# Retention and two dense layers on one core: a list scheduler with measured occupancies, a delay per engine, and VectorE that waits for GpSimd in its model

## The chip, the cores and the metric

The kernel runs on one core of one Trainium2 chip. The time is device microseconds of an execution of the program. Engines are TensorE (PE in the profile, its weight loads PEld), VectorE (DVE), ScalarE (ACT), GpSimd (POOL) and SyncE (SP), which issues every DMA.

## The reference

```python
# q, k, v: 4 batches x 8 heads x 576 positions x 64, float32
scores = (q @ k.T) / sqrt(64)
ret    = scores * gamma[h] ** (i - j)   (for i >= j, else 0)
x      = (ret @ v), heads side by side          # 2304 x 512
h = x @ w_in                                    # 512 x 2048
x = (h * tanh(log1p(exp(min(h, 20))))) @ w_out  # first layer
h = maximum(x @ w_in2, 0)
out = (h * h) @ w_out2                          # second layer
```

## The kernel before

**Stages.** Attention first: 20 steps (4 batches, each of 4 chunks of 128 positions and a tail of 64). A step has products `sc` (scores, line 394), `st` (state, 415) and `o` (438 and 446); VectorE multiplies the scores by a mask (402) and the output by a decay into `part` (464), ScalarE copies the state into `sbd`. Then the two layers. Each runs 4 passes over its hidden columns and in each pass 3 visits, one for 768 tokens. A visit has two rounds; a round makes the hidden block of 256 columns by seven products P1 to P7 (line 589, banks `h`) of 6 matmuls each, in the manner of Strassen, and `y_group` (639, banks `py`) multiplies activated blocks by the output weights.

**Numbers are split.** A float32 operand is kept as two tiles, a rounded part and the rest, and a product takes three matmuls. ScalarE writes the rounded part and another engine subtracts it to get the rest; that is a *split*. The splits of activations (`g`, line 237, always on VectorE) stand between `h` and `py`. The splits of weights (`win`, `wout`) and of the layer's input (`ring`) go through `either` (lines 229 to 231).

**Weights.** They arrive as 64-bit words in `raw`, two tiles in turn. `convert` (249) makes 32-bit floats of a block of 128 x 512: ScalarE forms `y` from the low words, VectorE masks, clamps and shifts the high words into `z` (261, 262, 263), puts the sign into `y` (264), and an integer add of `z` and `y` (265) ends it. Two `z` tiles are used in turn.

**After a product.** ScalarE copies a bank to `cp`, VectorE adds it to another bank (line 572) into a bank or, for P7, into the SBUF tile `e`. In the first layer ScalarE applies mish; in the second ScalarE takes a relu and VectorE multiplies (548). Then the split into `g`. When all columns of a pass are done, VectorE adds `py` to `part` (662). Between layers `sums_x` (317 to 319) and 324 form differences of blocks of `part`, and `split_x` fills the seven `ring` tiles, which `keep` writes to DRAM and `fetch` brings back for later passes.

**The planner.** No order is written out by hand. Every operation is first recorded in `Plan` with an engine, a cost and the names that it reads and writes. `due` gives each a latest time, counted back from TensorE's order; `order` then runs a list schedule over five queues, and the kernel is issued in the order of the planned starts. Each engine works its own queue strictly in that order. Some operations are shared (`ANY`): VectorE or GpSimd may take them (the integer add, the splits of weights and input), or ScalarE too (the scaling of v, line 380). Before the change VectorE takes a shared operation only when it is due within `SOON` of its start:

```python
                if e == "DVE":
                    c = [i for i in c if len(ops[i][0]) == 1 or due[i] + lag < max(free[e], ready[i]) + SOON]
```

One delay `LAT` stands between any two engines, and an engine's own results are free.

Of the kernel before, what the change touches and what calls it, by code (L numbers as in the profile page):

```python
# [19 lines left out]
DM = H * D  # L20
# [30 lines left out]
LAT = 0.2  # L51
AHEAD = 14
BACKLOG = 4.0
SOON = 2.0
# [3 lines left out]
class Plan:  # L58

# [12 lines left out]
    def add(self, eng, cost, fn, reads=(), writes=(), moved=0.0):  # L72
        i = len(self.ops)
        deps = set()
        for k in reads:
            deps.update(self.wrote.get(k, ()))
        for k in writes:
            deps.update(self.wrote.get(k, ()))
            deps.update(self.read.get(k, ()))
        deps.discard(i)  # L80
        for k in writes:
            self.wrote[k], self.read[k] = [i], []
        for k in reads:
            if k not in writes:
                self.read.setdefault(k, []).append(i)
        costs = cost if eng == "ANY" else {eng: cost}
        self.ops.append((costs, fn, sorted(deps), moved))
        return i

    def due(self):  # L90
        due = [1e9] * len(self.ops)
        t = 0.0
        for i, (costs, _, _, _) in enumerate(self.ops):
            if "PE" in costs:
                due[i] = t
                t += costs["PE"]
        for i in range(len(self.ops) - 1, -1, -1):
            for d in self.ops[i][2]:
                costs, _, _, moved = self.ops[d]
                c = min(costs.values()) + (moved + 2.0 if "SP" in costs else 0.0)  # L100
                due[d] = min(due[d], due[i] - c - LAT)
        return due

    def order(self):
# [21 lines left out]
        queue = lag = 0.0  # L126
        for _ in range(n):
            best = None
            while first < len(pe) and done_pe[first]:
                first += 1  # L130
            for e in self.ENGINES:
                c = waiting[e]
                if e == "PE":
                    c = [i for i in c if at[i] < first + AHEAD]
                if not c:
                    continue
                if e == "DVE":
                    c = [i for i in c if len(ops[i][0]) == 1 or due[i] + lag < max(free[e], ready[i]) + SOON]
# [10 lines left out]
            costs, fn, deps, moved = ops[i]  # L149
            for e in costs:  # L150
                waiting[e].remove(i)
            if eng == "PE":
                done_pe[at[i]] = True
                lag = now - due[i]
            start[i], on[i] = now, eng
            end = free[eng] = now + costs[eng]
            if eng == "SP":
# [11 lines left out]
    def issue(self, engines):  # L169
        for i in self.order():  # L170
            costs, fn, _, _ = self.ops[i]
            fn(engines[self.on[i]]) if len(costs) > 1 else fn()
# [3 lines left out]
def kernel(  # L176
# [45 lines left out]
    def act(out, in_, func=AF.Copy, n=512, reads=(), writes=(), **kw):  # L222
        fn = lambda: nc.scalar.activation(out() if callable(out) else out, in_() if callable(in_) else in_, func, **kw)  # L223
        plan.add("ACT", 0.2 + n * 0.00084, fn, reads, writes)
# [24 lines left out]
    def convert(i, after=()):  # L249
# [11 lines left out]
        dve(lambda: ts(z, hi, 0x7FFFFFFF, None, op0=band), 600, [kr + (1,)], [kz])  # L261
        dve(lambda: ts(zf, zf, HI_MIN, HI_MAX, op0=ALU.max, op1=ALU.min), 400, [kz], [kz])  # L262
        dve(lambda: ts(z, z, 3, None, op0=shl), 400, [kz], [kz])  # L263
        dve(lambda: stt(yu, hi, 0x80000000, yu, op0=band, op1=bor), 450, [kr + (1,), ky], [ky], True)  # L264
        add = lambda eng: eng.tensor_tensor(yu, z, yu, op=ALU.add)  # L265
        plan.add("ANY", dict(DVE=0.15 + DM * 0.0017, POOL=0.2 + DM * 0.0024), add, [kz, ky], [ky])
# [100 lines left out]
    def scale_v(s):  # L367
# [15 lines left out]
        plan.add("ANY", dict(DVE=1.2, POOL=1.25, ACT=2.1), fn, ["vdec", kl], [kl])  # L383
# [153 lines left out]
    def activate(m, key, ph, kp):  # L537
# [5 lines left out]
        else:  # L543
# [5 lines left out]
                TH, [kp, ("e", l)], [kp],  # L549
# [4 lines left out]
            TH, [kp, ("g", j, 0)], [("g", j, 1)],  # L554
        )

    def chain(u, fp):
# [18 lines left out]
        def product(name):  # L576
# [19 lines left out]
            plan.add("PE", 1.045, mm, [kw + (0,), kw + (1,), ("x", i, 0), ("x", i, 1), kb], [kb])  # L596
# [23 lines left out]
    def y_group(u, th, f):  # L620
# [7 lines left out]
        for i in range(na):  # L628
# [16 lines left out]
            plan.add("PE", 0.52 if m == 0 else 0.68, mm, [kw + (0,), kw + (1,), ("g", j, 0), ("g", j, 1), ky], [ky])  # L645
# [139 lines left out]
```

## Time and profile before

| | us |
|---|---|
| median of 3 runs | 867.67 (863.89 to 868.24) |
| the profiled execution | 865.53 |
| its span, first to last instruction | 863.8 |
| TensorE busy | 834.6 (97%) |
| VectorE, ScalarE, GpSimd busy | 594.7, 429.4, 296.8 |
| attention, to the first `h` product | 91.6 |

Busy time is what the records of an engine cover; matmul records overlap a little, and their ends are modelled. A record of VectorE is longer than its share of the engine's time by the overlap with the next one, some 0.1 us. The chain of waits names for each moment the work that the end hung on.

### The profile page before, as it was taken

How to read it: one execution, taken by the hardware profiler on the slowest of the kernel's cores; microseconds unless marked ns; L12 is line 12 of the kernel's file. 1: busy time of each engine (PE TensorE's matmuls, PEld its weight loads, DVE VectorE, ACT ScalarE, POOL GpSimd, SP SyncE). 2: the span in 40 equal slices, each digit the busy share in tenths (PEclk: the TensorE clock that was granted, in tenths of full speed). 3: DMA queues.
4: the chain of work that ended last, by engine and by line, in shares of the span. 5: the costliest groups of instructions: out<-in, count | busy, mean ns of one | idle time of the engine just before them, and what ended most of it. 6: DMA issues, size and time to landing. Idle time of an engine off the chain costs nothing.

```text
span 863.8 us, 13279 instructions
## 1 busy us (share of the span) xinstructions
PE 834.6 (97%) x5067; PEld 781.8 (91%) x5067; DVE 594.7 (69%) x969; ACT 429.4 (50%) x901; POOL 296.8 (34%) x194
## 2 busy tenths in 40 slices
PE   8789999999999999999999979999999999999998
PEld 6677898999999999999999868989889899889986
DVE  4999978557447853687469988678568874664553
ACT  4766675665345533553355646565344533443331
POOL 0655766444014401351039837442023411320000
PEclk9998999999999999999999989999999999999999
DMA  9999556377357547467528455468348546426621
GB/s 317 356 317 362 182 234 232 137 291 296 127 208 287 199 197 263 165 235 300 203 79 304 129 225 225 166 267 320 126 164 309 202 172 254 178 108 263 262 104 74
DMA packets 48079, 190.87 MB, mean 221 GB/s; under 512 B 9488, under 2 KB 11664, under 8 KB 48016
## 3 DMA queue, kind: packets, MB, share of 16 engines
q1 hardware_dynamic: 48016, 190.03, 59.2%
q8 instruction: 40, 0.66, 0.3%
q14 instruction: 23, 0.19, 0.1%
HBM read 152.26 MB, written 37.75 MB: 220 GB/s over the span
## 4 chain that ended last, share of the span: by engine, by line
PE 82%; DVE 12%; DMA 3%; issue 2%; ACT 1%; POOL 0%; SPq 0%; DVEq 0%; ACTq 0%; POOLq 0%
PE py L639 42%; PE h L589 36%; DMA qk<-in_qk_dram 2%; DVE z L261 2%; DVE z L262 1%; DVE y L264 1%; DVE g L237 1%; DVE z L263 1%; DMA qk<-in_qk_t_dram 1%; PE sc L394 1%; PE o L446 1%; PE o L438 1%; DVE a L402 1%; DVE part L662 1%; DVE part L324 1%
## 5 line engine op out<-in xcount | busy, mean ns | idle before, releaser
L589 PE MATMUL h<-ring,win 128*128 128x384 f32 x2016 | 385.7, 337 | 5.6 <-DVE e L572 2.1
L589 PEld LDWEIGHTS h<-ring,win 128*128 128x128 f32 x2016 | 356.4, 188 | 16.8 <-ACT cp L223 2.6
L639 PE MATMUL py<-wout,g 128*128 128x512 f32 x864 | 217.2, 396 | 5.7 <-DVE g L237 5.7
L639 PE MATMUL py<-g,wout 128*128 128x384 f32 x1152 | 215.1, 334 | 0.0
L639 PEld LDWEIGHTS py<-g,wout 128*128 128x128 f32 x1152 | 201.2, 188 | 0.2 <-DVE g L237 0.2
L639 PEld LDWEIGHTS py<-wout,g 128*128 128x128 f32 x864 | 162.2, 189 | 35.8 <-DVE g L237 6.1
L223 ACT ACTIVATE cp<-h 128x384 f32<-128x384 f32 x144 | 70.8, 492 | 135.9 <-PE h L589 134.9
L265 POOL TENSOR_TENSOR y<-z,y 128x512 uint32<-128x512 uint32 x64 | 87.3, 1365 | 145.7 <-DVE z L263 109.5
L230 POOL TENSOR_TENSOR win<-y,win 128x512 fp32r<-128x512 f32 x32 | 43.1, 1347 | 242.3 <-ACT win L223 242.3
L237 DVE TENSOR_TENSOR g<-h,g 128x384 fp32r<-128x384 f32 x144 | 78.9, 551 | 40.9 <-ACT g L223 40.8
L572 DVE TENSOR_TENSOR h<-h,cp 128x384 f32<-128x384 f32 x96 | 54.0, 562 | 55.7 <-PE h L589 52.2
L223 ACT ACTIVATE g<-h 128x384 fp32r<-128x384 f32 x144 | 70.6, 491 | 37.1 <-DVE h L548 35.0
L572 DVE TENSOR_TENSOR e<-h,cp 128x384 f32<-128x384 f32 x48 | 26.7, 556 | 82.8 <-ACT cp L223 82.8
L662 DVE TENSOR_TENSOR part<-py,part 128x384 f32<-128x384 f32 (+1 forms) x126 | 74.4, 611 | 9.2 <-PE py L639 7.8
L230 POOL TENSOR_TENSOR ring<-part,ring 128x768 fp32r<-128x768 f32 x30 | 61.5, 2061 | 10.2 <-ACT ring L223 10.1
L264 DVE SCALAR_TENSOR_TENSOR y<-raw,y 128x512 uint32<-128x512 uint32 x64 | 61.3, 961 | 2.8 <-ACT y L223 2.6
L223 ACT ACTIVATE h<-h 128x384 f32<-128x384 f32 x72 | 34.4, 478 | 53.4 <-DVE h L572 37.4
L223 ACT ACTIVATE e<-h 128x384 f32<-128x384 f32 x72 | 35.3, 490 | 51.4 <-DVE h L572 35.7
L237 DVE TENSOR_TENSOR g<-e,g 128x384 fp32r<-128x384 f32 x48 | 44.1, 919 | 21.0 <-ACT g L223 20.8
L230 POOL TENSOR_TENSOR wout<-y,wout 128x512 fp32r<-128x512 f32 x32 | 45.8, 1435 | 36.4 <-ACT wout L223 35.3
L548 DVE SCALAR_TENSOR_TENSOR h<-h,e 128x384 f32<-128x384 f32 x72 | 40.4, 561 | 20.0 <-ACT e L223 19.6
L223 ACT ACTIVATE y<-raw 128x512 f32<-128x512 uint32 x64 | 42.9, 672 | 18.2 <-POOL wout L230 6.1
(45 smaller groups left out, 668.9 us busy)
## 6 DMA issues: line engine op xcount, KB each, us to landing
ring<-d SPq DMA_DIRECT2D x126, 768.0 KB, 6.7
raw<-in_wp_dram SPq DMA_DIRECT2D x64, 512.0 KB, 5.7
d<-ring SPq DMA_DIRECT2D x42, 768.0 KB, 5.0
kv<-in_kv_dram SPq DMA_DIRECT2D x16, 512.0 KB, 7.1
qk<-in_qk_dram SPq DMA_DIRECT2D x16, 512.0 KB, 6.7
out_dram<-part SPq DMA_DIRECT2D x18, 256.0 KB, 2.0
qdec_sb<-in_qdec_dram SPq DMA_DIRECT2D x4, 256.0 KB, 7.9
qk<-in_qk_t_dram SPq DMA_DIRECT2D x4, 256.0 KB, 8.3
```

The lines of the kernel that those rows point to most:

```text
L223: fn = lambda: nc.scalar.activation(out() if callable(out) else out, in_() if callable(in_) else in_, func, **kw)
L230: fn = lambda eng: eng.tensor_tensor(out, a, b.bitcast(F32), op=op)
L237: return lambda: eng.tensor_tensor(out, a, b.bitcast(F32), op=ALU.subtract)
L261: dve(lambda: ts(z, hi, 0x7FFFFFFF, None, op0=band), 600, [kr + (1,)], [kz])
L262: dve(lambda: ts(zf, zf, HI_MIN, HI_MAX, op0=ALU.max, op1=ALU.min), 400, [kz], [kz])
L264: dve(lambda: stt(yu, hi, 0x80000000, yu, op0=band, op1=bor), 450, [kr + (1,), ky], [ky], True)
L265: add = lambda eng: eng.tensor_tensor(yu, z, yu, op=ALU.add)
L548: lambda: nc.vector.scalar_tensor_tensor(ph(), ph(), 0.0, e(), op0=ALU.max, op1=ALU.mult),
L572: lambda: nc.vector.tensor_tensor(dst(), bank(b)(), late["cp"][j], op=ALU.add),
L589: nc.tensor.matmul(dst(), w[:, hw, wi, s], ring[i][:, hx, k], start=(new and k == 0 and n == 0), stop=(k == 1 and n == 2), skip_group_chec ...
L639: nc.tensor.matmul(y, st[:, a], mv[:, b], start=(f == 0 and k == 0), stop=(f == FPP - 1 and k == 2), skip_group_check=True,)
L662: lambda dst=dst, y=y: nc.vector.tensor_tensor(dst, y(), dst, op=ALU.add),
```

## The change

The costs that the planner works with become occupancies (`0.07 + n * 0.00104` for any VectorE operation, `0.09 + n * 0.00084` for ScalarE). The one delay becomes one for each producing engine, `SEEN`, and only TensorE's own results are free. An operation may carry a mark `port`: it reads SBUF alone on VectorE. In the model such an operation starts on VectorE no earlier than 0.1 us ahead of the end of GpSimd's current one, and when VectorE chooses, a marked operation's due time is raised by that wait. The test with `SOON` and `lag` goes: VectorE may take a shared operation at any time, with its due time raised by `SPARE`.

```diff
-LAT = 0.2
+SEEN = dict(PE=0.2, ACT=0.15, DVE=0.13, POOL=0.1, SP=0.1)
-SOON = 2.0
+SPARE = 1.5
...
-                c = min(costs.values()) + (moved + 2.0 if "SP" in costs else 0.0)
-                due[d] = min(due[d], due[i] - c - LAT)
+                e = min(costs, key=costs.get)
+                c = costs[e] + SEEN[e] + (moved + 2.0 if e == "SP" else 0.0)
+                due[d] = min(due[d], due[i] - c)
...
-                if e == "DVE":
-                    c = [i for i in c if len(ops[i][0]) == 1 or due[i] + lag < max(free[e], ready[i]) + SOON]
-                    if not c:
-                        continue
...
-                i = min(can) if e == "PE" else min(can, key=lambda i: (due[i], i))
+                if e == "PE":
+                    i = min(can)
+                elif e == "DVE":
+                    held = max(0.0, free["POOL"] - now)
+                    i = min(can, key=lambda i: (due[i] + held * ops[i][4] + SPARE * (len(ops[i][0]) > 1), i))
+                else:
+                    i = min(can, key=lambda i: (due[i], i))
...
+            if eng == "DVE" and port:
+                now = max(now, free["POOL"] - 0.1)
             end = free[eng] = now + costs[eng]
...
-                ready[u] = max(ready[u], end + (0.0 if eng in ops[u][0] else LAT))
+                ready[u] = max(ready[u], end + (0.0 if eng == "PE" and "PE" in ops[u][0] else seen))
...
-        plan.add("DVE", 0.15 + n * (0.0017 if sbuf else 0.00105), fn, reads, writes)
+        plan.add("DVE", 0.07 + n * 0.00104, fn, reads, writes, port=sbuf)
...
-        plan.add("ANY", dict(DVE=0.15 + n * 0.0017, POOL=0.2 + n * 0.0024), fn, reads, writes)
+        plan.add("ANY", dict(DVE=0.07 + n * 0.00104, POOL=0.15 + n * 0.0024), fn, reads, writes, port=True)
...
-        plan.add("ANY", dict(DVE=0.15 + DM * 0.0017, POOL=0.2 + DM * 0.0024), add, [kz, ky], [ky])
+        plan.add("ANY", dict(DVE=0.6, POOL=1.4), add, [kz, ky], [ky], port=True)
...
-        plan.add("ANY", dict(DVE=1.2, POOL=1.25, ACT=2.1), fn, ["vdec", kl], [kl])
+        plan.add("ANY", dict(DVE=0.6, POOL=1.4, ACT=2.0), fn, ["vdec", kl], [kl], port=True)
```

The costs of the conversion's passes and of two TensorE operations change by small amounts too. The order of the instructions changes throughout. Lines of the changed kernel are one higher than those of the one before.

**VectorE in the first layer.** From an `h` add to the next `e` add, in the second visit; `z` are passes for later weight blocks, `ring` and L324 belong to the next input. Before:

```order
L572 TENSOR_TENSOR h<-h,cp 128x384
L261 TENSOR_SCALAR z<-raw 128x512
L262 TENSOR_SCALAR z<-z 128x512
L263 TENSOR_SCALAR z<-z 128x512
L237 TENSOR_TENSOR g<-h,g 128x384 x2
L261 TENSOR_SCALAR z<-raw 128x512
L262 TENSOR_SCALAR z<-z 128x512
L263 TENSOR_SCALAR z<-z 128x512
L324 TENSOR_TENSOR part<-part,t_96 128x2x384
L572 TENSOR_TENSOR e<-h,cp 128x384
```

after the change:

```order
L573 TENSOR_TENSOR h<-h,cp 128x384
L231 TENSOR_TENSOR ring<-part,ring 128x768
L238 TENSOR_TENSOR g<-h,g 128x384
L325 TENSOR_TENSOR part<-part,t_96 128x2x384
L231 TENSOR_TENSOR ring<-t_96,ring 128x768
L573 TENSOR_TENSOR e<-h,cp 128x384
```

The six passes on `z` have moved ahead of the `h` add, and two ring splits, which were GpSimd's, stand in their place.

**VectorE where the first layer goes over into the second.** From the last difference for the input (L324, now L325) to the second of two `h` adds. Before:

```order
L324 TENSOR_TENSOR part<-part,t_96 128x2x384
L572 TENSOR_TENSOR e<-h,cp 128x384
L264 SCALAR_TENSOR_TENSOR y<-raw,y 128x512
L263 TENSOR_SCALAR z<-z 128x512
L548 SCALAR_TENSOR_TENSOR e<-e 128x384
L548 SCALAR_TENSOR_TENSOR h<-h,e 128x384
L261 TENSOR_SCALAR z<-raw 128x512
L237 TENSOR_TENSOR g<-e,g 128x384
L237 TENSOR_TENSOR g<-h,g 128x384
L572 TENSOR_TENSOR h<-h,cp 128x384
```

after the change:

```order
L325 TENSOR_TENSOR part<-part,t_96 128x2x384
L573 TENSOR_TENSOR e<-h,cp 128x384
L231 TENSOR_TENSOR ring<-t_97,ring 128x768
L549 SCALAR_TENSOR_TENSOR h<-h,e 128x384
L549 SCALAR_TENSOR_TENSOR e<-e 128x384
L238 TENSOR_TENSOR g<-h,g 128x384
L573 TENSOR_TENSOR h<-h,cp 128x384
L318 TENSOR_TENSOR t_97<-part 128x768
L238 TENSOR_TENSOR g<-e,g 128x384
```

The passes on `y` and `z` between the `e` add and the `g` split from `e` have gone further down; a ring split has come in, and the wide difference `t_97` now stands ahead of the `g` split from `e`.

**GpSimd at the same place**, with the numbers of the tiles. Before:

```order
L230 TENSOR_TENSOR ring_75<-part_69,ring_75 128x768
L230 TENSOR_TENSOR ring_77<-t3_97,ring_77 128x768
L230 TENSOR_TENSOR ring_78<-part_69,ring_78 128x768
L230 TENSOR_TENSOR ring_74<-part_69,ring_74 128x768
L230 TENSOR_TENSOR win_80<-sums_95,win_80 128x768
L230 TENSOR_TENSOR win_80<-y_92,win_80 128x512
L265 TENSOR_TENSOR y_94<-z_90,y_94 128x512
L230 TENSOR_TENSOR wout_81<-y_93,wout_81 128x512
L265 TENSOR_TENSOR y_91<-z_89,y_91 128x512
L265 TENSOR_TENSOR y_92<-z_90,y_92 128x512
L230 TENSOR_TENSOR wout_82<-y_94,wout_82 128x512
L230 TENSOR_TENSOR wout_83<-y_91,wout_83 128x512
```

after the change:

```order
L231 TENSOR_TENSOR ring_76<-t2_96,ring_76 128x768
L231 TENSOR_TENSOR ring_75<-part_69,ring_75 128x768
L231 TENSOR_TENSOR ring_78<-part_69,ring_78 128x768
L231 TENSOR_TENSOR win_80<-y_92,win_80 128x512
L231 TENSOR_TENSOR ring_74<-part_69,ring_74 128x768
L231 TENSOR_TENSOR wout_81<-y_93,wout_81 128x512
L266 TENSOR_TENSOR y_91<-z_89,y_91 128x512
L231 TENSOR_TENSOR wout_82<-y_94,wout_82 128x512
L231 TENSOR_TENSOR wout_83<-y_91,wout_83 128x512
```

Between the same tiles `ring_75` and `wout_83` one ring split, a split of `sums` and two integer adds are no longer GpSimd's at this place.

## Rows read from the trace of the kernel before

**Rows 1.** Table by stage; columns: stretch, length, then busy time (instructions) by engine.
```profile
50.00:75.00 25.00, 20.52 (x289) 17.57 (x289) 24.29 (x35) 13.03 (x36) 13.36 (x10) 0.90 0.99 365
91.00:106.00 15.00, 12.99 (x71) 11.90 (x70) 14.87 (x21) 9.60 (x19) 12.40 (x8) 1.00 0.40 127
130.00:148.00 18.00, 15.95 (x92) 15.63 (x91) 15.43 (x16) 9.53 (x18) 12.31 (x7) 1.00 0.73 277
148.00:450.00 302.00, 302.00 (x1735) 302.00 (x1734) 184.07 (x329) 146.73 (x292) 85.10 (x60) 0.99 0.57 214
450.00:503.00 53.00, 46.72 (x255) 43.79 (x253) 52.21 (x59) 31.48 (x58) 48.96 (x26) 0.97 0.62 226
530.00:859.00 329.00, 329.00 (x1630) 295.26 (x1629) 209.42 (x368) 143.13 (x289) 75.13 (x51) 1.00 0.53 201
```

**Rows 2.** Chain of waits in order of time: start, length, what.
```profile
91.62 2.37 PE h L589 x12
...
154.31 2.08 PE h L589 x12
...
582.74 2.08 PE py L639 x9
...
849.76 8.90 PE py L639 x39
```

**Rows 3.** Groups by line and shape, TensorE: busy, mean | idle before.
```profile
L589 PE MATMUL h<-ring,win 128*128 128x384 f32 x2016 | 385.7, 337 | 5.6 <-DVE e L572 2.1 <-DVE g L237 1.5 <-ACT cp L223 1.3
...
L639 PE MATMUL py<-wout,g 128*128 128x512 f32 x864 | 217.2, 396 | 5.7 <-DVE g L237 5.7
L639 PE MATMUL py<-g,wout 128*128 128x384 f32 x1152 | 215.1, 334 | 0.0
```

**Rows 4.** TensorE in order of time: start, length, group [idle before].
```profile
147.25 4.98 PE L589 MATMUL h<-ring,win 128*128 128x384 f32 x18 [2.05 <-DVE e L572]
...
502.92 4.21 PE L639 MATMUL py<-wout,g 128*128 128x512 f32 x9 [5.74 <-DVE g L237]
```

**Rows 5.** Groups by line and shape, VectorE and GpSimd.
```profile
L237 DVE TENSOR_TENSOR g<-h,g 128x384 fp32r<-128x384 f32 x144 | 78.9, 551 | 40.9 <-ACT g L223 40.8
...
L230 POOL TENSOR_TENSOR ring<-part,ring 128x768 fp32r<-128x768 f32 x30 | 61.5, 2061 | 10.2 <-ACT ring L223 10.1
...
L264 DVE SCALAR_TENSOR_TENSOR y<-raw,y 128x512 uint32<-128x512 uint32 x64 | 61.3, 961 | 2.8 <-ACT y L223 2.6
...
L263 DVE TENSOR_SCALAR z<-z 128x512 uint32<-128x512 uint32 x64 | 44.1, 689 | 0.9
L237 DVE TENSOR_TENSOR g<-e,g 128x384 fp32r<-128x384 f32 x48 | 44.1, 919 | 21.0 <-ACT g L223 20.8
```

**Rows 6.** VectorE in order of time, between the layers.
```profile
451.64 1.49 DVE L290 TENSOR_TENSOR sums<-y,sums 128x256 f32<-128x256 f32 x1
...
494.21 2.06 DVE L263 TENSOR_SCALAR z<-z 128x512 uint32<-128x512 uint32 x1
...
500.24 2.15 DVE L237 TENSOR_TENSOR g<-e,g 128x384 fp32r<-128x384 f32 x1
...
503.73 0.94 DVE L317 TENSOR_TENSOR t<-part 128x768 f32<-128x768 f32 x1
```

**Rows 7.** VectorE in order of time, first layer.
```profile
128.96 0.69 DVE L264 SCALAR_TENSOR_TENSOR y<-raw,y 128x512 uint32<-128x512 uint32 x1
...
134.90 0.57 DVE L572 TENSOR_TENSOR h<-h,cp 128x384 f32<-128x384 f32 x1 [0.96 <-PE h L589]
...
145.44 0.43 DVE L263 TENSOR_SCALAR z<-z 128x512 uint32<-128x512 uint32 x1
...
146.65 0.55 DVE L572 TENSOR_TENSOR e<-h,cp 128x384 f32<-128x384 f32 x1
```

**Rows 8.** VectorE and TensorE in order of time, attention.
```profile
66.67 3.96 DVE L261 TENSOR_SCALAR z<-raw 128x512 uint32<-128x512 uint32 x1
...
72.91 2.08 PE L394 MATMUL sc<-qk 64*128 64x128 f32 x16 [0.50 <-DMA qk<-in_qk_dram]
```

More of the change, by code (lines that the diff above doesn't have):

```diff
@@ L70, in __init__, with add @@
         self.ops, self.wrote, self.read = [], {}, {}
-    def add(self, eng, cost, fn, reads=(), writes=(), moved=0.0):
+    def add(self, eng, cost, fn, reads=(), writes=(), moved=0.0, port=False):
         i = len(self.ops)
@@ L86, in add @@
         costs = cost if eng == "ANY" else {eng: cost}
-        self.ops.append((costs, fn, sorted(deps), moved))
+        self.ops.append((costs, fn, sorted(deps), moved, port))
         return i
@@ L92, in due @@
         t = 0.0
-        for i, (costs, _, _, _) in enumerate(self.ops):
+        for i, (costs, *_) in enumerate(self.ops):
             if "PE" in costs:
@@ L98, in due @@
             for d in self.ops[i][2]:
-                costs, _, _, moved = self.ops[d]
-                c = min(costs.values()) + (moved + 2.0 if "SP" in costs else 0.0)
-                due[d] = min(due[d], due[i] - c - LAT)
+                costs, _, _, moved, _ = self.ops[d]
+                e = min(costs, key=costs.get)
+                c = costs[e] + SEEN[e] + (moved + 2.0 if e == "SP" else 0.0)
+                due[d] = min(due[d], due[i] - c)
         return due
@@ L125, in order @@
                 release(i)
-        queue = lag = 0.0
+        queue = 0.0
         for _ in range(n):
@@ L148, in order @@
             now, i, eng = best
-            costs, fn, deps, moved = ops[i]
+            costs, fn, deps, moved, port = ops[i]
             for e in costs:
@@ L153, in order @@
                 done_pe[at[i]] = True
-                lag = now - due[i]
             start[i], on[i] = now, eng
+            if eng == "DVE" and port:
+                now = max(now, free["POOL"] - 0.1)
             end = free[eng] = now + costs[eng]
+            seen = SEEN[eng]
             if eng == "SP":
@@ L170, in issue @@
         for i in self.order():
-            costs, fn, _, _ = self.ops[i]
+            costs, fn, *_ = self.ops[i]
             fn(engines[self.on[i]]) if len(costs) > 1 else fn()
@@ L223, in act @@
         fn = lambda: nc.scalar.activation(out() if callable(out) else out, in_() if callable(in_) else in_, func, **kw)
-        plan.add("ACT", 0.2 + n * 0.00084, fn, reads, writes)
+        plan.add("ACT", 0.09 + n * 0.00084, fn, reads, writes)
     def dve(fn, n, reads, writes, sbuf=False):
-        plan.add("DVE", 0.15 + n * (0.0017 if sbuf else 0.00105), fn, reads, writes)
+        plan.add("DVE", 0.07 + n * 0.00104, fn, reads, writes, port=sbuf)
     def either(op, out, a, b, n, reads, writes):
         fn = lambda eng: eng.tensor_tensor(out, a, b.bitcast(F32), op=op)
-        plan.add("ANY", dict(DVE=0.15 + n * 0.0017, POOL=0.2 + n * 0.0024), fn, reads, writes)
+        plan.add("ANY", dict(DVE=0.07 + n * 0.00104, POOL=0.15 + n * 0.0024), fn, reads, writes, port=True)
     def dma(out, in_, reads, writes, size):
@@ L595, in product @@
             kb = ("h", banks[b])
-            plan.add("PE", 1.045, mm, [kw + (0,), kw + (1,), ("x", i, 0), ("x", i, 1), kb], [kb])
+            plan.add("PE", 1.041, mm, [kw + (0,), kw + (1,), ("x", i, 0), ("x", i, 1), kb], [kb])
             if name == "P1":
@@ L643, in mm @@
                     )
-            plan.add("PE", 0.52 if m == 0 else 0.68, mm, [kw + (0,), kw + (1,), ("g", j, 0), ("g", j, 1), ky], [ky])
+            plan.add("PE", 0.52 if m == 0 else 0.69, mm, [kw + (0,), kw + (1,), ("g", j, 0), ("g", j, 1), ky], [ky])
         if f < FPP - 1:
```

12 lines of the change are left out of this document (6 added, 6 removed).

## Prediction

> **What bounds the kernel now.** I read the table by stage first, then the chain of waits, then the rows of the engines where those two point. From 148 to 450 us and from 530 to 859 us TensorE is busy without a gap and VectorE only six tenths of the time [rows 1]: nothing that VectorE or GpSimd do there moves the end. Three other stretches of the two layers lose time, and each has VectorE busy nearly throughout: 91 to 106 (14.87 of 15 us), 130 to 148 (15.43 of 18) and 450 to 503 (52.21 of 53) [rows 1].
>
> How much is lost follows from rates. In the chain an undisturbed group of 12 h products takes 2.08 us, 0.1733 each, and 9 of the wide py products take 2.08, 0.2311 each [rows 2]. With the counts of [rows 3], (2016 + 1152) x 0.1733 + 864 x 0.2311 = 748.7 us. The two layers run from 91.62 to 858.66, the end of the last py group [rows 2], so 767.0 us: 18.3 are lost. At 147.25 TensorE had waited 2.05 us and then ran 18 products in 4.98 instead of 3.12 us [rows 4]: 3.9. Idle time from 450 to 503 is 6.3 us [rows 1], of it 5.74 in one wait that ends at 502.92, with a group of 9 at 4.21 instead of 2.08 behind it [rows 4]: 8.4, and about 3.5 more in small pieces up to 530. Some 2.5 us are left for 91 to 106.
>
> Why VectorE is late there is in the length of its rows. A shift of a weight block takes 0.43 us at 145.44 [rows 7] and 2.06 at 494.21; the g split that reads e takes 2.15 at 500.24 [rows 6]. Long rows read SBUF alone; the g split averages 0.92 us from e and 0.55 from h, which lies in PSUM [rows 5]. The long ones end where a GpSimd instruction ends, and GpSimd was busy 48.96 of these 53 us [rows 1]. So VectorE is **held** while GpSimd works. Between 451.64 and 500.24 I count 22 held instructions (first and last in [rows 6]) that take 24 us beyond their shortest rows, of the 52 us that VectorE was busy. A held instruction is no loss by itself; the loss is that adds and splits that TensorE needs stand behind it in VectorE's order.
>
> **The change part by part.** *Moved work.* Counted in the program's order, 59 of 190 instructions leave GpSimd and 58 reach VectorE (9 ring, 24 win and 8 wout splits, 17 integer adds; one v scaling goes to ScalarE). Priced by their groups, 2.06 us for a ring split [rows 5] and 1.35 to 1.9 for the others, GpSimd loses about 93 us, near a third of its time.
>
> What an integer add costs on VectorE no row shows: it is a custom instruction over 1024 two-byte elements. The bounds are 0.69 us, a two-input pass of 512 four-byte elements that is not held [rows 7], and 1.25, the 0.94 of a 768-wide pass [rows 6] scaled to 1024. I take 0.7, since the bytes are those of 512 words, and keep 1.25 for the range. Splits go by the same rows: 0.95 for 768 elements, 0.69 for 512.
>
> *450 to 530* carries most of the sum. From the first ring split of this visit to the last of the next, GpSimd's order has 24 instructions before and 16 after. If held time goes with their number, 24 x 16 / 24 = 16 us are left: 8 saved. VectorE's own work for the same stretch of TensorE's order hardly changes, 27.4 before and 27.0 us after by unheld prices: four splits come in, and passes for later weight blocks go out behind the g splits. Between the e add and the g split from e stood three weight passes; after, a ring split and one wide difference stand there, and no weight pass. VectorE's 52 us become about 43.5, and TensorE needs 43 for these products: the 5.74 us wait shrinks to about 1, and the slow group behind it goes (2.1). What is deferred comes back: behind 503 VectorE's own work rises by 1 to 4 us with as much on GpSimd as before, so those small pieces stay and may grow by 1. Gain 7, from 3 (half the held time stays) to 10.
>
> *130 to 148.* Between the h add at 134.9 and the e add that starts at 146.65 [rows 7] stood six weight passes, with five ring splits on GpSimd beside them; after the change no weight pass stands there but two ring splits on VectorE, with two on GpSimd. Own work 3.8 us and at most two holds of 2: under 8 against 11.7. Wait and slow clock should go: 3.5 of 3.9, at worst 1.
>
> *91 to 106.* Own work goes from 9.7 to 8.9 us, GpSimd's from 13.5 to 12.9 by shortest prices. Gain 1, from 0 to 2.
>
> *0 to 91, attention.* VectorE is busy 24.29 of 25 us [rows 1], so every moved instruction shows. Four more shared ones run on it, 3.0 us (4.2 at the upper price); GpSimd goes from 28 instructions to 24, the fewer ones mostly between 60 and 78, where one pass was held 3.96 us and TensorE ran a 16-product group at 2.08 [rows 8], at about half speed. Held time saved is 3 to 4 us, and 4 more if the slow clock goes. Against that, the DMA share is 0.99 from 50 to 75 [rows 1], and SP's order has eight weight blocks and six ring copies ahead of the last attention loads both before and after; the swap of the first two loads hides behind the mask's landing. I take 2 us gained, from 3 lost to 5 gained.
>
> *Delays and occupancies* add no instruction; they act through these orders. Small new waits somewhere: 1.5 us lost.
>
> Sum: 2 + 1 + 3.5 + 7 - 1.5 = 12 us off the profiled execution's 865.5: 853.5. That execution lies 2 us below the median of the three runs, which spread over 4.4; for the median after I say **854.5**.
>
> The Trainium skill speaks against such a move: "Perfetto Trace Analysis", section "Optimizing Scalar/DVE Operations", says that GpSimd and VectorE share a port under an exclusive lock, so that offloading between the two might not help. By that rule nothing is gained and the time stays near 865.
>
> Sums over the program look like that too. The three SBUF groups of [rows 5] alone are held 54 us beyond their shortest rows, all such groups about 107, that is 0.36 per us of GpSimd; 93 us less there frees some 34, and the moved work costs 45 to 54 on VectorE. I go by the stretches, where 16 replace 24 at equal own work, and not by the average; the trade is the first rival.
>
> **Rivals.** *VectorE trades held time for own work and stays late.* For it: the sums just given, and more than half of GpSimd's loss lies where TensorE is saturated anyway. Against it: VectorE's own work from 450 to 503 does not rise. Then the place at 130 to 148 improves and the one behind 503 worsens by about as much, and the median's own offset of 2 stays: 862 to 867, say 864.5.
>
> *Moved instructions are held themselves.* 17 of them stand in the stretches from 91 to 160 and 450 to 560. If each takes what held rows take, 2.1 us [rows 6], that is 36 us of VectorE in front of adds for TensorE, against a third of some 38 held, 12.6. VectorE has perhaps 14 us to spare in them, so the end moves out by 9: 875, **slower**. It decides from about 1.6 us per moved instruction, where 27 equals 12.6 and the spare time. For it: rows of 2 us are common. Against it: the planner now adds the rest of GpSimd's instruction to the due time of work that would be held, so other work goes ahead.
>
> *All of it.* The three stretches lose nothing and attention gains 4: 18.3 + 4 less 1 off, 844 to 848.
>
> **How the numbers follow.** The forecast, 848 to 861 by its bounds, has 0.56; all of it 0.12; the trade 0.23; slower 0.09. About 0.5% (4.3 us) is what a measurement can tell from no change, so faster means below 863.3. The forecast, the full case and a quarter of the trade are that: 0.74. The rest of the trade is within: 0.17. The range, 846 to 867, leaves out the slow case and most of the full one.
>
> **What would show it.** Right: the wait before the py group near 500 falls below 2 us; held instructions on VectorE from 450 to 500 fall from 22 to about 15; the wait before 18 h products near 145 is gone; GpSimd's busy time is near 205 us; the first h product starts between 87 and 92. An integer add at 0.7 confirms the price, 1.25 the upper one. Wrong: splits on VectorE that average over 1.6 us; the same wait, only later, at 510 to 560; a first h product after 95; gaps between 148 and 450, where I expect none.

## The result and the profile after

The change takes 857.12 us (median of 4 runs, 856.17 to 858.28) against 867.13 (863.89 to 868.24): a ratio of 0.9891 [0.9861, 0.9922], faster by 1.1%. (The numbers in brackets are a 95% interval.) The profiled execution took 856.53, 9.0 less than that of before. Its table by stage, with the columns of [rows 1]:

```profile
25.00:50.00 25.00, 21.55 (x273) 18.76 (x274) 22.80 (x34) 23.16 (x71) 18.93 (x11) 0.86 1.01 370
91.00:106.00 15.00, 13.05 (x75) 12.85 (x76) 12.63 (x20) 8.67 (x18) 10.75 (x8) 0.77 0.27 78
130.00:148.00 18.00, 18.00 (x105) 18.00 (x105) 14.34 (x24) 11.25 (x22) 3.73 (x2) 1.00 0.58 222
148.00:450.00 302.00, 302.00 (x1745) 302.00 (x1744) 193.99 (x357) 145.99 (x289) 44.72 (x32) 1.00 0.59 219
450.00:503.00 53.00, 52.57 (x285) 49.80 (x284) 52.93 (x66) 33.83 (x64) 33.68 (x18) 1.00 0.62 238
503.00:530.00 27.00, 25.90 (x129) 22.96 (x128) 25.16 (x35) 16.63 (x31) 20.87 (x12) 1.00 0.54 212
```

TensorE's idle time from 130 to 148 is gone, and from 450 to 503 it is 0.43 us (before 6.28, [rows 1]). Over the program GpSimd is busy 212.3 us instead of 296.8. But VectorE is as busy from 450 to 503 as it was: 52.93 for 52.21. TensorE's waits in the layers (start, length, group, idle before it and what ended that) are short now, where [rows 4] had 5.74:

```profile
94.67 13.14 PE L590 MATMUL h<-ring,win 128*128 128x384 f32 x60 [1.35 <-DVE part L465]
...
495.66 2.31 PE L640 MATMUL py<-wout,g 128*128 128x512 f32 x9 [0.30 <-DVE g L238]
...
528.40 2.34 PE L640 MATMUL py<-wout,g 128*128 128x512 f32 x9 [1.10 <-DVE g L238]
```

The first row is the other side of the account: the first `h` product starts at 94.67, not at 91.62 [rows 2], and its 60 matmuls take 13.14 us where 60 x 0.1733 = 10.4 would do; the granted clock from 91 to 106 averages 0.77 of full speed, so that TensorE ran part of this stretch at the lower of its two levels (1.2 GHz instead of 2.4). The chain's last row gives the end of the layers:

```profile
840.75 8.90 PE py L640 x39
```

So the layers run from 94.67 to 849.65, 755.0 us: 6.3 above the 748.7 that the counts need, where 18.3 were lost before. Gained in the layers 12.0, lost in attention 3.05: the 9.0. Each of these figures comes from one execution of each kernel; how far executions differ in attention is told in the last section. The groups that answer to [rows 5], and that of the moved integer adds (busy, mean ns):

```profile
L265 DVE SCALAR_TENSOR_TENSOR y<-raw,y 128x512 uint32<-128x512 uint32 x64 | 54.5, 852 | 3.0 <-ACT y L224 3.0
L264 DVE TENSOR_SCALAR z<-z 128x512 uint32<-128x512 uint32 x64 | 37.4, 587 | 1.1
L238 DVE TENSOR_TENSOR g<-e,g 128x384 fp32r<-128x384 f32 x48 | 34.2, 712 | 21.2 <-ACT g L224 21.2
L266 DVE CUSTOM_DVE_ANT_0 y<-z,y 128x1024 uint16<-128x1024 uint16 x17 | 14.2, 834 | 0.5
```

Rows are held less, but not much less: from 450 to 503 I count 18 held ones with 19.8 us beyond their shortest rows, where it was 22 with 24. From 450 to 530 it is 28 us, and 27 before: there nothing was saved. That the layers became 12 us shorter all the same is what the experiments had to explain.

### The profile page after: what moved, and what is told of

The parts are those of the page before. It is cut to its first block, busy times and chain, and to the rows that moved or that the text cites. A ratio compares the mean times of both kernels' runs of the same rounds, so it can differ in the third digit from the quotient of the medians.

```text
span 854.7 us, 13229 instructions
## 1 busy us (share of the span) xinstructions
PE 835.0 (98%) x5067; PEld 784.9 (92%) x5067; DVE 608.4 (71%) x1027; ACT 431.6 (50%) x909; POOL 212.3 (25%) x135
## 4 chain that ended last, share of the span: by engine, by line
PE 85%; DVE 10%; DMA 2%; issue 1%; ACT 1%; SPq 1%; POOL 0%; DVEq 0%; ACTq 0%
PE py L640 43%; PE h L590 38%; DMA raw<-in_wp_dram 2%; DVE y L265 1%; PE st L416 1%; PE o L447 1%; DVE part L465 1%; DVE ring L231 1%; DVE g L238 1%; DVE part L663 1%; DVE a L403 1%; SPq L235 1%; PE o L439 1%; DVE win L231 1%; DVE part L319 0%
## 5 line engine op out<-in xcount | busy, mean ns | idle before, releaser
L640 PE MATMUL py<-wout,g 128*128 128x512 f32 x864 | 214.7, 393 | 1.4 <-DVE g L238 1.4
L266 POOL TENSOR_TENSOR y<-z,y 128x512 uint32<-128x512 uint32 x47 | 68.7, 1463 | 208.4 <-DVE y L265 151.4
L231 POOL TENSOR_TENSOR win<-y,win 128x512 fp32r<-128x512 f32 x20 | 27.9, 1397 | 230.1 <-ACT win L224 230.1
L231 POOL TENSOR_TENSOR ring<-part,ring 128x768 fp32r<-128x768 f32 x26 | 54.6, 2106 | 28.7 <-ACT ring L224 28.6
L265 DVE SCALAR_TENSOR_TENSOR y<-raw,y 128x512 uint32<-128x512 uint32 x64 | 54.5, 852 | 3.0 <-ACT y L224 3.0
L238 DVE TENSOR_TENSOR g<-e,g 128x384 fp32r<-128x384 f32 x48 | 34.2, 712 | 21.2 <-ACT g L224 21.2
L231 POOL TENSOR_TENSOR wout<-y,wout 128x512 fp32r<-128x512 f32 x24 | 35.8, 1495 | 25.9 <-ACT wout L224 25.9
```

The costliest lines, as they stand in the source:

```text
L238: return lambda: eng.tensor_tensor(out, a, b.bitcast(F32), op=ALU.subtract)
L640: nc.tensor.matmul(y, st[:, a], mv[:, b], start=(f == 0 and k == 0), stop=(f == FPP - 1 and k == 2), skip_group_check=True,)
```

## The experiments

Three numbers are read from each run's profile: the first `h` product; what the layers lose (end of the last row of the chain, less the first `h` product, less 748.7); and, counted in the program's order on VectorE, how many passes of weight blocks that the planner wants from 530 us on stand ahead of the `g` splits that lie just before 500 us in the layers (the row 498.66 of the first experiment, below). The count depends on where the 530 is put (from 510 us on it is 18 before and 10 after the change), but the difference of 7 or 8 does not; and it tells of one place, not of all that the layers lose. Some expectations give layers by the modelled end of the matmuls, 1.1 to 1.3 us more. Where they say 135 instructions on GpSimd after the change, four that the planner does not order are counted in; it is 131 for 190. Ratios are to the kernel before in the same set of runs; its median there is 865.1 to 865.8, in the table it stands with its first set.

| kernel | GpSimd | weight passes ahead | layers lose | first h | us |
|---|---|---|---|---|---|
| before | 190 | 8 | 18.3 | 91.62 | 867.13 |
| the change | 131 | 1 | 6.3 | 94.67 | 857.12 |
| old sharing rule, wait kept | 190 | 2 | 4.3 | 93.67 | 856.38 |
| no wait, new sharing rule | 97 | 22 | 30.0 | 98.63 | 885.02 |
| no wait, old sharing rule | 190 | 22 | 35.3 | 100.46 | 891.61 |
| mean hold for the wait | 189 | 18 | 19.5 | 99.03 | 874.62 |
| wait, no choice term | 133 | 1 | 5.2 | 94.72 | 856.06 |
| before, with sharing rule | 138 | 0 | 9.9 | 97.30 | 862.81 |
| nothing on GpSimd | 0 | 6 | 3.9 | 91.61 | 852.31 |
| before, nothing on GpSimd | 0 | 0 | 25.9 | 88.27 | 868.40 |

### Which part does it

**The sharing rule taken out.** On the kernel after:

```diff
+                if e == "DVE":
+                    c = [i for i in c if len(ops[i][0]) == 1 or due[i] + lag < max(free[e], ready[i]) + SOON]
...
-due[i] + held * ops[i][4] + SPARE * (len(ops[i][0]) > 1)
+due[i] + held * ops[i][4]
```

> The change without its sharing rule: VectorE takes shared work by the old rule (only if it is due within 2 us), the new occupancies, delays and the model of VectorE waiting for GpSimd stay. Counted in the program's order GpSimd has 190 instructions again, as before the change (after it: 135), 34 of them in the 84 us of TensorE work that hold the wait near 500 us (before 36, after 28). Theory, fewer GpSimd instructions make the gain: the wait near 500 us is back at 3 to 6 us, VectorE's rows are held as before, and the time is 862 to 868. Rival, the order that counts what would be held makes the gain: the adds and splits that TensorE needs go ahead although as much is held, the wait near 500 stays below 1.5 us, and the time is 856 to 859.

856.38 us (853.68 to 858.01), 0.9893 [0.9872, 0.9914]: the whole gain, with GpSimd as full as before. My theory of fewer GpSimd instructions fell. VectorE's rows here, in order of time, around the one wait that is left near 500, and that wait (1.37 us):

```profile
493.00 1.27 DVE L243 TENSOR_TENSOR g<-e,g 128x384 fp32r<-128x384 f32 x1
494.19 0.55 DVE L243 TENSOR_TENSOR g<-h,g 128x384 fp32r<-128x384 f32 x1
494.65 0.55 DVE L578 TENSOR_TENSOR h<-h,cp 128x384 f32<-128x384 f32 x1
495.12 1.65 DVE L323 TENSOR_TENSOR t<-part 128x768 f32<-128x768 f32 x1
...
498.66 1.01 DVE L243 TENSOR_TENSOR g<-h,g 128x384 fp32r<-128x384 f32 x2
...
494.79 2.32 PE L645 MATMUL py<-wout,g 128*128 128x512 f32 x9 [1.37 <-DVE g L243]
```

Rows are held all the same: 21 from 450 to 503, by 20.6 us. But only adds, multiplies, splits and the differences of the layer's input stand here, no pass of a weight block.

What a pass costs there is read in the kernel before. From the `e` add to the `g` split that ends TensorE's wait of 5.74 us, with the rows 494.21 and 500.24 of [rows 6] at their places:

```profile
491.94 0.54 DVE L572 TENSOR_TENSOR e<-h,cp 128x384 f32<-128x384 f32 x1
492.41 1.88 DVE L264 SCALAR_TENSOR_TENSOR y<-raw,y 128x512 uint32<-128x512 uint32 x1
...
496.19 2.17 DVE L548 SCALAR_TENSOR_TENSOR e<-e 128x384 f32<-128x384 f32 x1
498.29 0.55 DVE L548 SCALAR_TENSOR_TENSOR h<-h,e 128x384 f32<-128x384 f32 x1
498.75 1.56 DVE L261 TENSOR_SCALAR z<-raw 128x512 uint32<-128x512 uint32 x1
...
502.32 0.55 DVE L237 TENSOR_TENSOR g<-h,g 128x384 fp32r<-128x384 f32 x1
```

and the same after the change, where the wait is 0.30:

```profile
490.40 0.55 DVE L573 TENSOR_TENSOR e<-h,cp 128x384 f32<-128x384 f32 x1
490.87 2.14 DVE L231 TENSOR_TENSOR ring<-t,ring 128x768 fp32r<-128x768 f32 x1
492.94 0.55 DVE L549 SCALAR_TENSOR_TENSOR h<-h,e 128x384 f32<-128x384 f32 x1
493.40 1.74 DVE L549 SCALAR_TENSOR_TENSOR e<-e 128x384 f32<-128x384 f32 x1
495.06 0.55 DVE L238 TENSOR_TENSOR g<-h,g 128x384 fp32r<-128x384 f32 x1
```

VectorE is never idle in either. From the start of the `e` add to the end of the split it takes 10.93 us before and 5.21 after. By the starts of the rows the three weight passes that are gone took 5.27 of it, and the `g` split from `e`, which now stands behind, 2.08; the ring split that came in takes 2.07. So the order of VectorE accounts for this wait, though what stands there is held in both kernels.

**The wait taken out.**

```diff
-            if eng == "DVE" and port:
-                now = max(now, free["POOL"] - 0.1)
```

and the term `held * ops[i][4]` with it.

> The change without its model of VectorE waiting for GpSimd: the sharing rule, the occupancies and the delays stay. Counted in the program's order GpSimd has 97 instructions (135 with the model), 19 instead of 28 in the 84 us around 500 us, and VectorE 1062 instead of 1027. Theory, fewer GpSimd instructions make the gain: held time falls further, no wait over 1 us is left near 500, and the time is 852 to 857, not above the change's. Rival, the order that counts what would be held makes the gain: waits come back in the dense stretches (130 to 148, 450 to 530) and the time is 860 to 867.

885.02 us (884.16 to 886.58), 1.0234 [1.0219, 1.0248]: slower than either kernel, with fewer instructions on GpSimd than either. Waits came back, and cost more than the rival said.

**Neither sharing rule nor wait**, the occupancies and delays alone:

> The change with neither its sharing rule nor its model of VectorE waiting for GpSimd: the new occupancies and delays alone. GpSimd has 190 instructions. The run without the model but with the sharing rule took 885.02. If the short occupancies without the waits did that (the planner believes VectorE free while it is held), this takes 875 to 895, ScalarE's copies of h being late for TensorE again. If it was the sharing rule that overfilled VectorE, this takes 857 to 868.

891.61 us (890.73 to 892.25), 1.0304 [1.0288, 1.0319]. So it is not the sharing rule that overfills VectorE. What happens shows at one place. VectorE:

```profile
504.35 0.55 DVE L575 TENSOR_TENSOR h<-h,cp 128x384 f32<-128x384 f32 x1
504.81 0.67 DVE L292 TENSOR_TENSOR sums<-sums,y 128x256 f32<-128x256 f32 x1
505.41 2.03 DVE L294 TENSOR_TENSOR y<-y 128x256 f32<-128x256 f32 x1
507.37 0.41 DVE L293 TENSOR_TENSOR sums<-y,sums 128x256 f32<-128x256 f32 x1
507.70 0.55 DVE L551 SCALAR_TENSOR_TENSOR h<-h,e 128x384 f32<-128x384 f32 x1
```

GpSimd, ScalarE and TensorE there:

```profile
503.24 3.92 POOL L233 TENSOR_TENSOR ring<-part,ring 128x768 fp32r<-128x768 f32 x2
...
508.29 0.49 ACT L226 ACTIVATE g<-h 128x384 fp32r<-128x384 f32 x1 [2.30 <-DVE h L551]
508.68 0.48 ACT L226 ACTIVATE cp<-h 128x384 f32<-128x384 f32 x1
...
509.30 1.91 PE L592 MATMUL h<-ring,win 128*128 128x384 f32 x5 [3.51 <-ACT cp L226]
```

Three sums of a weight block, which by the planner's due times have some 70 us longer than the multiply at 507.70, stand ahead of it. One of them, 0.41 us when free, is held to 507.44 by two `ring` splits that end at 507.16. Behind the multiply ScalarE's split waits 2.30, behind that its copy of another bank, and TensorE waits 3.51 for the copy. Held time is not what differs: from 450 to 530 I count 26 held rows by 25.8 us, and 31 by 31.7 in the first experiment. What differs is what stands behind them. By the planner's short occupancies VectorE had time to spare, and it filled it with what was ready: 22 weight passes ahead of the `g` splits, against 2. For the passes of a weight block the occupancies fell by more than the "small amounts" of the section on the change: their four costs summed to 2.84 us before and sum to 1.61 now.

Both this run and the one with the wait have the new delays as well as the new occupancies, and no run takes these two apart. The planner by itself can be asked for its order: short occupancies with the old delay put 20 weight passes ahead, the old costs with the new delays 9. So the occupancies make the order; what either of these two kernels takes was not measured, nor the old occupancies with the wait.

**A mean in place of the wait:**

```diff
-                now = max(now, free["POOL"] - 0.1)
+                now += 0.21
```

> The run with occupancies alone (891.61), with one number more: the planner adds 0.21 us to each instruction of VectorE that is marked as held by GpSimd, at any time, in place of the wait for GpSimd's end. 0.21 is the mean in the run with the wait and the old sharing rule: some 89 us held over 418 marked instructions. Same 190 instructions on GpSimd. If the planner only has to know how much VectorE is held, this takes 855 to 860, as with the wait (856.38). If it has to know when (a held row of 2 us in a dense stretch), waits of TensorE come back there and it takes 865 to 885.

874.62 us (874.07 to 876.90), 1.0113 [1.0094, 1.0131]. The mean wins back 17 of the 35 us between the run without and the run with the wait, and no more: 18 weight passes still stand ahead. Holds are not spread evenly; in the first experiment 20.6 of some 89 us lie in these 53 us. Here the planner has to know when, not only how much.

**The wait without the choice term:**

```diff
-due[i] + held * ops[i][4] + SPARE * (len(ops[i][0]) > 1)
+due[i] + SPARE * (len(ops[i][0]) > 1)
```

> The change with the wait for GpSimd kept in VectorE's planned time, but without the term that lets other work go ahead of what would be held. Counted in the program's order nearly nothing moves (GpSimd 133 instructions for 131, VectorE 1025 for 1027). If the planned time is what the model gives: 856 to 859, as the change. If the choice is: 862 to 885.

856.06 us (853.76 to 857.16), 0.9887 [0.9869, 0.9906]: as the change. The planned time does it. (The term without the wait was not run: it puts every engine in the same order as with neither.)

**The sharing rule on the kernel before:**

> The kernel before with the sharing rule alone: VectorE takes shared work whenever nothing of its own is due by 1.5 us earlier; the old occupancies, one delay for all engines and no model of holding. Counted in the program's order GpSimd has 138 instructions and VectorE 1022, about as after the whole change (135 and 1027), 22 of GpSimd's in the 84 us around 500 us (after the change 28). Theory, fewer GpSimd instructions make the gain: 855 to 860. Rival, the order that counts holds, or the measured occupancies: 862 to 868, with the wait near 500 above 3 us.

862.81 us (861.16 to 863.10), 0.9968 [0.9957, 0.9980]: a small gain, by its time the rival's; but the wait above 3 us that the rival named near 500 did not come (0.44 at 497.6, 0.97 at 524.7). It has as few weight passes ahead as the change and loses 9.9 us in the layers instead of 18.3, but its first `h` product comes at 97.30. So the rule alone is a second way to some 8 of the 12 us in the layers; whether it gets there by fewer instructions on GpSimd or by the order that comes with them, this run does not tell. It adds nothing to the wait: the change with and without the rule takes the same time.

### Without GpSimd

**Every shared operation on VectorE** (a v scaling on ScalarE too):

```diff
-dict(DVE=0.07 + n * 0.00104, POOL=0.15 + n * 0.0024)
+dict(DVE=0.07 + n * 0.00104)
-dict(DVE=0.6, POOL=1.4), add
+dict(DVE=0.6), add
-dict(DVE=0.6, POOL=1.4, ACT=2.0)
+dict(DVE=0.6, ACT=2.0)
```

> The change with GpSimd taken out of the shared work: every split, integer add and v scaling goes to VectorE (a v scaling may go to ScalarE as well), 1159 instructions on VectorE and none on GpSimd. It isolates the hold: with nothing on GpSimd no row of VectorE that reads and writes SBUF should be held, so shifts at 0.43, the g split from e at about 0.55 and the 768-wide difference near 0.94 us every time. By unheld prices VectorE's own work is then 78 us for the 84 us of TensorE around 500 us (57 after the change), 48 for the first 55 us of the layers and 77 for the some 93 us of attention. Theory, held rows are what made VectorE late: it is on time with more work of its own, no wait above 1.5 us in the layers, and the time is 850 to 858. Rival, held time is traded for own work one for one: VectorE stays as late as before, 862 to 870. A third reading, that rows are long for another cause than GpSimd: they stay at 2 us, VectorE is overfull around 500 us, and the time is above 875.

852.31 us (850.96 to 853.82), 0.9852 [0.9836, 0.9868], better than the change. The same groups as above:

```profile
L266 DVE SCALAR_TENSOR_TENSOR y<-raw,y 128x512 uint32<-128x512 uint32 x64 | 44.0, 689 | 4.2 <-ACT y L225 4.1
L265 DVE TENSOR_SCALAR z<-z 128x512 uint32<-128x512 uint32 x64 | 27.1, 424 | 0.7
L239 DVE TENSOR_TENSOR g<-e,g 128x384 fp32r<-128x384 f32 x48 | 26.8, 557 | 20.9 <-ACT g L225 20.8
L232 DVE TENSOR_TENSOR ring<-t,ring 128x768 fp32r<-128x768 f32 x12 | 11.4, 953 | 0.7 <-ACT ring L225 0.7
L267 DVE CUSTOM_DVE_ANT_0 y<-z,y 128x1024 uint16<-128x1024 uint16 x64 | 43.9, 687 | 0.5
```

and the stage from 450, with the columns of [rows 1]:

```profile
450.00:503.00 53.00, 53.00 (x287) 50.51 (x286) 53.00 (x99) 34.88 (x65) 0.00 (x0) 1.00 0.64 246
```

No row is held any more: the means are the shortest rows of before, 424 ns for a shift that averaged 689 [rows 5]. That the hold comes from GpSimd is shown. (Weight passes stand ahead here too, 6 of them, but at 0.42 or 0.69 us each TensorE does not wait for them.) VectorE does 99 instructions in the 53 us in which it did 59 [rows 1], and TensorE does not wait once.

**The same on the kernel before**, with the old occupancies:

> The kernel before with nothing changed but that GpSimd takes no shared work: old occupancies, one delay. By those occupancies VectorE has 88 us of work for the 84 us of TensorE around 500 us, so the planner believes that it is late there; on the chip it would have 78. Theory, what is held in front of needed work costs the time: with no hold left it is 850 to 856 whatever the planner believes. Rival, the planner's picture of VectorE's time has to be right: it puts work in the wrong order, waits of TensorE over 3 us in all come back in the layers, and the time is 858 to 875.

868.40 us (865.86 to 870.58), 1.0035 [1.0023, 1.0048]: the rival's. Nothing is held here either, so the 16 us between this and the last run come from the order, that is from the planner's numbers: occupancies, delays, and its rule for the v scalings, which were changed together. Around 500 TensorE is hardly late (52.18 of 53 us busy). The loss lies at the start of the layers, where the old occupancies add up to 84.6 us of VectorE's work for 55 of TensorE's (48 by the new ones). TensorE waits there for `ring` tiles, among others:

```profile
103.44 4.79 PE L590 MATMUL h<-ring,win 128*128 128x384 f32 x18 [2.79 <-ACT h L224]
...
119.42 0.44 PE L590 MATMUL h<-ring,win 128*128 128x384 f32 x1 [3.31 <-ACT ring L224]
120.58 1.97 PE L590 MATMUL h<-ring,win 128*128 128x384 f32 x5 [0.72 <-DVE ring L231]
```

Why the planner put the `ring` splits so late I have not taken apart. That it is the slow clock of VectorE in the plan, and not the delays, is likely but not shown. With no weight pass ahead near 500 and 25.9 us lost, this run also shows that the count of the table is no measure of the whole.

### Attention

Here is ScalarE in the kernel after, around 40 us, and what TensorE waits for:

```profile
40.00 2.01 ACT L382 ACTIVATE kv<-kv,vdec_sb 128x64 f32<-128x64 f32 x8
42.03 0.78 ACT L224 ACTIVATE sbd<-st 64x256 f32<-64x256 f32 x2
42.84 2.02 ACT L382 ACTIVATE kv<-kv,vdec_sb 64x64 f32<-64x64 f32 x8
...
42.86 1.12 PE L416 MATMUL st<-kv 128*64 128x64 f32 x16 [2.80 <-ACT sbd L224]
43.91 2.08 PE L439 MATMUL o<-qk,sbd 128*128 128x128 f32 x8
...
30.51 1.16 PE L439 MATMUL o<-qk,sbd 128*128 128x128 f32 x8
```

A v scaling of eight instructions stands ahead of the two copies into `sbd`; TensorE waits 2.80 us, and its next group of 8 takes 2.08 us where it took 1.16 at 30.51 (granted clock 0.70 from 40 to 45 us, 1.00 from 30 to 35). **ScalarE out of the scalings:**

```diff
-dict(DVE=0.6, POOL=1.4, ACT=2.0)
+dict(DVE=0.6, POOL=1.4)
```

> The change with ScalarE taken out of the choice for the v scalings: in the program's order 5 of the 20 go to VectorE and 15 to GpSimd (after the change 2, 3 and 15 on ScalarE); the 84 us around 500 us are as after the change. Reading A, attention ends 3 us later after the change because ScalarE takes v scalings of 2.0 us ahead of the sbd copies that TensorE waits for (2.8 us at 42.86): the first h product comes at 88 to 92 instead of 94.67, the time is 852 to 855. Reading B, loads set the end of attention: the first h product stays at 93 to 96 and the time at 856 to 858. Reading C, GpSimd's 15 scalings hold VectorE there: first h product after 96, time 859 or more.

850.90 us (849.45 to 852.86), 0.9832 [0.9812, 0.9852], with the first `h` product at 88.92 and the layers as after the change (6.6 lost): reading A's numbers, and a little more than it said. The way there is not quite reading A's. From 25 us to the first `h` product TensorE waits 0.4 us for `sbd` copies where it waited 4.1 after the change, but it waits for GpSimd's scalings instead (4.9), and its idle time is 9.5 us for 10.0. What is shorter is its busy time, 54.4 us for 59.7, at a higher granted clock (0.95 from 25 to 50 us for 0.86, 1.00 from 50 to 75 for 0.93). That the time falls without ScalarE's scalings is shown by the medians, every run here below every run of the change; that the clock rose because of them is not.

**No GpSimd and no ScalarE:**

> The version without GpSimd (852.31 us) with all 20 v scalings on VectorE: neither GpSimd nor ScalarE takes one. VectorE's own work up to the first h product is 81 us by unheld prices, against 77. Reading A (ScalarE's scalings delay the sbd copies): first h product at 87 to 90 instead of 91.61, time 848 to 851. Reading B (loads set it): 91 to 93 and 851 to 853. Reading C (VectorE, 81 us of work in 90, becomes the bound of attention): first h product after 93.5, time above 854.

852.98 us (852.13 to 854.24), 0.9859 [0.9843, 0.9875]. First `h` product at 94.22: reading C by its place, VectorE is the bound in this execution (busy throughout from 50 to 91, and `st` waits for its scalings seven times, 11.3 us); the layers lose only 3.0, so the time is B's.

### Put together

> GpSimd keeps the v scalings of attention and nothing else (17 of 20; VectorE 3, ScalarE none); every split and integer add is VectorE's. It puts together the layers of the version without GpSimd (753.9 us from the first h product to the last py product) and the attention of the version without ScalarE's scalings (first h product at 88.92). If attention and layers add up, the first h product comes at 88 to 91 and the time is 847 to 850, under both. Rival: with the ring splits of attention on VectorE as well (70 us of its own work by unheld prices, held by GpSimd's scalings) VectorE becomes the bound there: first h product after 93, time 852 to 855.

850.77 us (850.22 to 853.13), 0.9839 [0.9819, 0.9859]. The layers lose 2.8, as hoped, but the first `h` product comes at 92.44, near the rival's. TensorE's idle time from 25 us up to it is 9.7 us, as good as in the run at 850.90 (9.5), so here too the clock makes most of the difference. The last run lets GpSimd take all shared work recorded ahead of the first `h` product and none behind:

```diff
+    def shared_on(d, p):
+        return dict(DVE=d, POOL=p) if len(plan.ops) < ATTENTION else dict(DVE=d)
...
-dict(DVE=0.07 + n * 0.00104, POOL=0.15 + n * 0.0024)
+shared_on(0.07 + n * 0.00104, 0.15 + n * 0.0024)
```

with `ATTENTION = 342`, the integer add in the same way, and the v scalings on VectorE or GpSimd.

> GpSimd takes shared work in attention (33 instructions before the first h product, the v scalings not on ScalarE, as in the run at 850.9) and none behind it (all splits and integer adds of the layers on VectorE, as in the version without GpSimd). The order up to the first h product is that of the run at 850.9, where it came at 88.92; the layers of the two versions without GpSimd took 752.8 and 753.9 us. If the stretches add up: first h product at 88 to 90, time 847 to 849.5. Rival: the 52 us of own work that VectorE has for the first 55 us of the layers, started 3 us earlier with less done ahead, make it late there: waits of over 1 us between 91 and 148, time 850 to 854.

846.89 us (845.81 to 851.76), 0.9787 [0.9768, 0.9806]: the lowest median, where the change has 0.9891, and 3.9 us under the run before it with the same layers. By these medians GpSimd is of use for the splits of attention too. Its profiled execution, 851.76, is the slowest of the five:

```profile
92.83 12.27 PE L595 MATMUL h<-ring,win 128*128 128x384 f32 x60 [0.80 <-DVE part L470]
```

Layers 2.9 lost and no wait in them. If the median's layers take as long, its first `h` product comes near 88 (92.83 less 851.76 - 846.89); no profile shows it.

## Why the prediction was right, and where it was wrong

The time, 857.12 for 854.5, and the sign are as forecast; the layers gained 12.0 where 10 were summed up, attention lost 3.05 where 2 were to be gained. That the places and the order were read rightly is no luck; that the sum came so near is in part luck, since its largest term was priced by held time, which stayed, and two errors of opposite sign met. Two rows of the kernel before that are used below, with the columns of [rows 1]:

```profile
25.00:50.00 25.00, 20.16 (x298) 17.40 (x295) 24.54 (x32) 19.57 (x58) 16.88 (x11) 1.00 0.92 344
503.00:530.00 27.00, 26.03 (x118) 22.75 (x119) 21.14 (x37) 13.83 (x27) 7.47 (x6) 0.92 0.43 161
```

- **450 to 530.** The wait near 500 went from 5.74 to 0.30 with 1.10 at 528.40, and the slow group went, as said; of the 12.0 us some 8 are gained here, where 7 were forecast. The step "If held time goes with their number, 24 x 16 / 24 = 16 us are left" failed. Held time fell by 4 us up to 503 and not at all up to 530, VectorE's 52 us became 52.93, not 43.5, and the run with the old sharing rule has the gain without any fewer instructions on GpSimd. The count itself did not fall by time: behind 503, where I expected "as much on GpSimd as before", there are 12 instructions for the 6 before, so that 450 to 530 has 30 for 32. What I had noted beside it and not priced, that no weight pass stands between the `e` add and the `g` split any more, is what the rows of both kernels show in its place: 5.27 us of passes gone from ahead of a wait that fell by 5.44.
- **130 to 148.** 3.5 forecast, and the place is clean: 18.00 of 18 us.
- **91 to 106 and attention.** "I take 2 us gained" came out as 3.05 lost, just past the lower bound of 3, and the first `h` product missed the 87 to 92 that were to show it. "Held time saved is 3 to 4 us" came true (19.6 us before, 14.3 after), but the end of attention did not follow it: from 25 us to the first `h` product TensorE is idle 10.0 us in both kernels, of it 3.8 before and 4.1 after for copies into `sbd`. The 3.1 us are in its busy time, 56.6 before and 59.7 after. The slow clock, "4 more if the slow clock goes", did not go; it came earlier: 0.86 from 25 to 50 us after the change, 1.00 before. Whether the change does this or the one execution of each kernel stays open: the last section has two executions of one order that differ by 3.9 us in the same way, and the medians, 10.0 apart, put the loss nearer 2. ScalarE's v scalings, which take 5 to 6 us with them when they go, can be little of it, since 14 of the 15 were there before and TensorE waited as long for the copies. Nor did 91 to 106 gain its 1: some 2.5 us were lost there before, and 13.14 - 10.4 = 2.7 now, in the slow clock behind attention.
- **Delays and occupancies** "add no instruction; they act through these orders", 1.5 us lost. They are the largest lever here: without the wait the short occupancies and new delays cost 3.0%, with it they give the gain.
- **The integer add.** 0.687 us free, the 0.7 that I took; its mean of 0.834 in the change is the hold.
- **The trade** (0.23) did not come: VectorE stayed as busy, but TensorE did not wait for it. The rule of the Trainium skill that stood beside it ("Perfetto Trace Analysis", section "Optimizing Scalar/DVE Operations") says that moving work between the two engines might not help, since they share a port under a lock. The lock agrees with the runs (424 ns for 689 without GpSimd). Whether it helped hung on the plan: moving all of it gave 0.9852 with the new numbers and 1.0035 with the old ones.
- **Moved instructions held themselves** came nearer than one mean tells: the 41 moved splits average 1.11 us, but the 16 moved instructions that I count in its two stretches (91 to 160 and 450 to 560) average 1.42, against the 1.6 from which it decides, and the five splits of the second stretch 2.18. The end did not move out, so VectorE had the room.
- **Gaps between 148 and 450**: none, as expected.

## What to carry to other kernels

A list scheduler fills what it believes to be idle time, so an engine that it believes free too early puts work that nobody needs yet in front of work that is needed now; a contention that stretches instructions belongs in its clock as a wait at the moment, not as a mean; here short occupancies without it were worse than long ones. Held time on an engine is no loss until something needed stands behind it: count what stands there, in the program's order, before pricing the hold. Where a slow helper holds a fast engine, try the kernel without the helper, stage by stage.

## What the runs showed that I had not expected

Two kernels with the same order on every engine up to the first `h` product reached it at 88.92 and 92.83 in the executions that were profiled. The granted clock from 25 to 50 us was 0.95 in the one and 0.80 in the other, and 1.00 and 0.86 from 50 to 75. TensorE's idle time from 25 us on was 9.5 and 9.2 us, its busy time 54.4 and 58.6. So a single profile places the end of attention to some 4 us here, and only medians decide about it; the layers repeat to a tenth of that (751.5 and 751.6 in the last two versions).
